# Two loads moved to the queue of ScalarE and a stored Gram block laid out by head, in a kernel of linear attention, soft experts and a feed-forward network

## The chip, the cores and the metric

The kernel runs on one core of one Trainium2 chip. The metric is the time of one launch in device microseconds (us); smaller is better. Three runs of the kernel before took 604.23, 604.43 and 599.4 us (median 604.23). A further execution was recorded by the hardware profiler: 600.38 us, with a span of 598.7 us between its first and last instruction. All rows shown before the result are of that execution.

The engines are TensorE (PE, with its weight loads as PEld), VectorE (DVE), ScalarE (ACT), GpSimd (POOL) and SyncE (SP). SP does no arithmetic here: before the change it issues all DMAs.

## The reference, cut to what matters

Three parts follow one another: a delta-rule attention (4 batches, 8 heads, 768 tokens, head size 48), a soft mixture of experts (8 experts with 4 slots each) and a feed-forward network on 3072 rows.

```python
def _attn_ref(q, k, v, beta):
    k_n = k / (np.linalg.norm(k, axis=-1, keepdims=True) + 1e-06)
    state = np.zeros((B, H, D, D))
    for t in range(S):
        kt, vt, bt = k_n[:, :, t], v[:, :, t], beta[:, :, t, None]
        y[:, :, t] = np.einsum('bhd,bhde->bhe', q[:, :, t], state)
        v_old = np.einsum('bhde,bhd->bhe', state, kt)
        state = state + bt[..., None] * np.einsum('bhd,bhe->bhde', kt, vt - v_old)

def _moe_ref(x, phi, w1, w2):          # x: 3072 x 384
    logits = x @ phi
    d = softmax(logits, axis=0)         # over the tokens
    slot_input = (d.T @ x).reshape(8, 4, 384)
    slot_out[e] = np.maximum(slot_input[e] @ w1[e], 0) @ w2[e]
    return softmax(logits, axis=1) @ slot_out

def _moe2_ref(x, w_in, w_out):
    h = x @ w_in
    return np.maximum(0.01 * h, h) @ w_out
```

## The kernel before, in words

The 768 tokens are cut into 24 chunks of 32, the steps `s` of the loop. All 32 (batch, head) pairs are worked on at once, half of the heads in each of two halves `A`. Inside a chunk the recurrence is a triangular system; its inverse is needed per pair and per chunk. Four chunks make a group `g`.

**Ahead of the recurrence.** `gram(s)` multiplies a chunk's keys with its keys and queries on PE (L189). ACT copies the key part out of PSUM into `gcs` (L196), a tile of one group that lies in the shared buffer `arena`; DVE masks the other part into `mm` (L205). Once the four Gram blocks of a group are there, `solve(g)` transposes the stored copy on DVE so that each pair lies on a partition (L229), eliminates column by column (some 120 short DVE operations, L269, L283 and L287 most of them), transposes back (L290) and stores the inverse as two fp16 parts `tc` (L294 on ACT, L295 on DVE). In the trace these tiles appear as `arena`. Grams run eight chunks ahead of the recurrence; the last is issued in step 15.

**One step of the recurrence.** `ks(A)` on PE (L377) applies the state to the keys, `z_of` splits the result into three fp16 parts (L391 and L392 on ACT, L393 on DVE), `u_mm` multiplies by the inverse `tmb` (L399) and ACT rounds to `u` (L404, then L407 after a correction on PE, L406; from step 17 on DVE L409 does the second part), `s_mm` adds to the state (L420, copied to `st` by ACT, L423), `mu_mm` makes the output `y` (L430), and ACT and DVE store it as `xg` (L736, L737). The next step's `ks(0)` needs `st` of half 0. Beside that, POOL scales the values (`vs`, L327) and splits keys (L337), ACT prepares the keys (L333, L336), and the soft mixture works on groups of finished rows (`soft`, L450 to L503).

**Loads of one step.** All go through SP's queue in the order that the scheduler gives it: the pair of loads `kqb` (keys and queries in block form, 192 KB each, L351), `kv` (keys and values four steps ahead, 384 KB, L304), four copies `tmb` of the inverse (L355), four copies `khb` of the split keys (L344), two `arena` loads and one `kqr` load for the Gram block of ten steps ahead (L172, L178). `kqb`, `tmb` and `khb` have two halves, used by even and odd steps. `load_kv(s + 4, ...)` is held until the last matmul of `u` of half 0. In the later steps weights of the stages behind (768 KB each, L519, L557) are issued on the same queue, each when a slot comes free.

Every DMA takes the next of eight semaphores, whichever queue it is on, and before it is issued it waits until the DMA eight places earlier in the program has landed. An engine works its queue strictly in order, so what stands behind a waiting DMA waits too.

**What sets the order.** A scheduler orders the instructions of each engine from their dependences and a cost estimate; `behind(...)`, `tc.issue_after(...)` and `pri(...)` narrow its choice. Dividing a tile differently or moving a load thus also shifts other instructions.

Of the kernel before, what the change touches and what calls it, by code (L numbers as in the profile page):

```python
# [8 lines left out]
F32 = mybir.dt.float32  # L9
# [3 lines left out]
AF = mybir.ActivationFunctionType  # L13
# [4 lines left out]
NST = 24  # L18
# [29 lines left out]
def fused_kernel(ctx: ExitStack, tc: tile.TileContext, kq, kv, bu, phi, w1, w2, wi, wo, out):  # L48
    nc = tc.nc
    ve, sc, gp, pe, sy = nc.vector, nc.scalar, nc.gpsimd, nc.tensor, nc.sync  # L50
# [15 lines left out]
    kqb = [free_a.tile(KQT, F32, name=f"kqb{i}") for i in range(2)]  # L66
# [29 lines left out]
    def place(kb, shape, dt):  # L96
        n = 1
        for x in shape[1:]:
            n *= x
        n = n // (1 if dt == F32 else 2)  # L100
        v = arena[0:shape[0], 256 * kb:256 * kb + n]
        v = v if dt == F32 else v.bitcast(dt)
        if len(shape) == 2:
            return v
        d = "abcdef"[:len(shape) - 1]
        return v.rearrange(f"p ({' '.join(d)}) -> p {' '.join(d)}", **dict(zip(d, shape[1:])))
# [3 lines left out]
    AT = {"gc": 32, "gu": 44, "R": 48, "tmp": 52}  # L110
# [41 lines left out]
    def behind(*keys):  # L152
        st = ExitStack()
        for k in keys:
            if k in end:
                st.enter_context(tc.issue_after(end[k]))
        return st

    kqc, gcs, mms, tcs, nns, kvs, vns = {}, {}, {}, {}, {}, {}, {}
# [22 lines left out]
    def gram(s, later=None):  # L182
        k = s % 2
        c, kb = kqc[s // 2]
        gp_, tg = ((ps_g, "gm"), (ps_x, "xp"), (ps_y, "y"), (ps_m, "m"))[s % 4 if s < GALT else 0]
        gm = gp_.tile([128, 8, 64], F32, tag=tg, name="gm")
        for h in range(8):
            for bp in range(2):
                end["gm"] = pe.matmul(gm[64 * bp:64 * bp + 64, h, :], kb[:, k, bp, :, h], c[:, k, bp, :, :, h],  # L189
                                      start=(h == 0), stop=True, skip_group_check=True).ins  # L190
            if h % 4 == 3:
                yield
        if s % 4 == 0:
            gcs[s // 4] = place(AT["gc"], [128, 4, 8, 32], F32)
        with behind("nu") if s > 3 else nullcontext():
            gc_ = sc.activation(gcs[s // 4][:, s % 4], gm[:, :, 0:32], AF.Copy).ins  # L196
        if s < 4:
            end["gc"] = gc_
        m = p_mm.tile([128, 2, 32, 4], F32, tag="mm", name="mm")
        mms[s] = m  # L200
        mv = m.rearrange("p a i h -> p a h i")
        gv = gm[:, :, 32:64].rearrange("p (a h) i -> p a h i", a=2)

        def mask():
            ve.tensor_tensor(mv, gv, causal.unsqueeze(1).unsqueeze(1).to_broadcast([128, 2, 4, 32]), MULT)  # L205

        if later is None:
            mask()
        else:
            later.append(mask)  # L210
        yield
# [13 lines left out]
    def solve(g):  # L225
        gc = gcs.pop(g)
        tcg = p_late.tile([128, 4, 4, 2, 32, 4], F16, tag=f"tc{g % 2}", name="tc", bufs=1)
        gu = place(AT["gu"], [128, 32, 32], F32)
        ve.transpose(out=gu, in_=gc.rearrange("p s h i -> p i (s h)"))  # L229
        yield  # L230
        nu, ru, br, er, t0 = [p_gs.tile([128, 32], F32, tag=n, name=n) for n in ("nu", "ru", "br", "er", "t0")]
        nn = p_gs.tile([128, 4, 8], F32, tag="nn", name="nn")
        R = place(AT["R"], [128, 32, 32], F32)
        dg = diag(gu)

        end["t0"] = ve.tensor_scalar(t0, dg, 2.0 ** -63, None, MAX).ins
        sc.activation(nu, t0, AF.Ln)
        end["nu"] = sc.activation(nu, nu, AF.Exp, scale=0.5).ins

        ve.tensor_scalar(er, nu, 2e-6, 1e-12, MULT, ADD)  # L240
        ve.tensor_tensor(er, er, dg, ADD)
        ve.reciprocal(er, er)
        ve.scalar_tensor_tensor(br, er, -1.0, beta[:, g, :], MULT, MULT)
        ve.tensor_scalar(diag(R), br, 64.0, None, MULT)
        nns[g], tcs[g] = nn, tcg
        yield
        for m in (16, 8, 4, 2, 1):
            q = below(AT["gu"], m)
            rows = br.rearrange("p (b x) -> p b x", x=2 * m)[:, :, m:2 * m].unsqueeze(3).to_broadcast([128, 16 // m, m, m])
            ve.tensor_tensor(q, q, rows, MULT)  # L250
            if m > 4:
                yield
        yield
        for m in (16, 8, 4, 2, 1):
            cols = diag(R).rearrange("p (b x) -> p b x", x=2 * m)[:, :, 0:m].unsqueeze(2).to_broadcast([128, 16 // m, m, m])
            ve.tensor_tensor(below(AT["R"], m), below(AT["gu"], m), cols, MULT)
            if m > 4:
                yield

        ve.reciprocal(ru, nu)  # L260
        ve.tensor_tensor(ru, ru, dg, MULT)
        ve.tensor_tensor(nu, nu, ru, ADD)
        ve.tensor_scalar(t0, nu, -32.0, -64e-6, MULT, ADD)
        ve.transpose(out=nn.rearrange("p s h -> p (s h)"), in_=t0)
        yield
        tmp = place(AT["tmp"], [128, 1024], F32)

        def row(i, j):
            ve.scalar_tensor_tensor(R[:, i, 0:j], R[:, j, 0:j], gu[:, i, j:j + 1], R[:, i, 0:j], MULT, ADD)  # L269

        for j in range(1, 31):
            n, w = 30 - j, j
            if w <= COLS:
                for k in reversed(range(w)):
                    ve.scalar_tensor_tensor(R[:, j + 1:, k], gu[:, j + 1:, j], R[:, j, k:k + 1], R[:, j + 1:, k], MULT, ADD)
                yield
            elif n < ROWS:
                for i in range(j + 1, 32):
                    row(i, j)
                yield  # L280
            else:
                tv = tmp[:, 512 * (j % 2):512 * (j % 2) + n * w].rearrange("p (i k) -> p i k", i=n)
                ve.tensor_tensor(tv, gu[:, j + 2:, j:j + 1].to_broadcast([128, n, w]),  # L283
                                 R[:, j:j + 1, 0:w].to_broadcast([128, n, w]), MULT)
                row(j + 1, j)
                yield
                ve.tensor_tensor(R[:, j + 2:, 0:w], R[:, j + 2:, 0:w], tv, ADD)  # L287
                yield
        tt = place(AT["tmp"], [128, 8, 32, 4], F32)
        ve.transpose(out=tt.rearrange("p s i h -> p i s h"), in_=R)  # L290
        tt = tt.rearrange("p (s a) i h -> p s (a i h)", a=2)
        th, tl = [tcg[:, :, i].rearrange("p s a i h -> p s (a i h)") for i in range(2)]
        for k in (slice(0, 1), slice(1, 4)):
            sc.activation(th[:, k], tt[:, k], AF.Copy, scale=2.0 ** -11)  # L294
            solved[g] = ve.scalar_tensor_tensor(tl[:, k], th[:, k], -2048.0, tt[:, k], MULT, ADD).ins  # L295
        yield

    solved = {}

    def load_kv(s, ins=None):  # L300
        p, k = divmod(s, 2)
        if k == 0:
            kvs[p] = p_late.tile([128, 2, 2, 384], F32, tag=f"kv{p % 2}", name="kv", bufs=1)
        d = sy.dma_start(kvs[p][:, k], kv[p, :, k])  # L304
        if ins is not None:
            hold(d, ins)
        return d
# [32 lines left out]
    def step_kdma(s):  # L340
        khc = khs.pop(s)
        for b in range(4):
            q, o = slice(32 * b, 32 * b + 32), 48 * (b % 2)
            last_dma[0] = sy.dma_start(khb[q, s % 2, :, :, b // 2, o:o + 48, :].rearrange("p l a d h -> p (l a) (d h)"), khc[q]).ins  # L344

    def step_dma(s):
        g, k = divmod(s, 4)
        if s:
            for sl in range(2):
                q, i = slice(48 * sl, 48 * sl + 48), slice(32 * sl, 32 * sl + 32)  # L350
                sy.dma_start(kqb[s % 2][q, :, :, i].rearrange("p b x i h -> p (b x) (i h)"),  # L351
                             kq[s // 2, q, s % 2].rearrange("p (c y) -> p c y", c=4))
        for b in range(4):
            q = slice(32 * b, 32 * b + 32)
            sd = sy.dma_start(tmb[s % 2][q, :, :, q, :].rearrange("p l a i h -> p (l a) (i h)"), tcs[g][q, k].rearrange("p l a i h -> p (l a) (i h)"))  # L355
        last_dma[0] = sd.ins
# [9 lines left out]
    last_u = {}  # L366
# [286 lines left out]
    for s in range(NST):  # L653
        y = ps_y.tile([128, 8, 48], F32, tag="y", name="y")
# [3 lines left out]
        def ks(A):  # L658
            if s:
                ks_mm(s, A)  # L660
            z[A] = z_of(s, A) if s else first_z[A]
# [11 lines left out]
                drain(gram(s + GA))  # L673
        with behind("gm", "k"):
            ks(1)
        if s in (3, 7, 11, 15):
            bs.add(solve(s // 4 + 2))
        if s + 1 < NST:
# [22 lines left out]
        with behind("y"):  # L701
# [14 lines left out]
            if s < NST - 1:  # L716
                with pri("st"):
                    s_mm(s, 1, u[1])
        if s + 4 < NST:
            load_kv(s + 4, last_u[0].ins)  # L720
        if s + 1 < NST - 1:
            with pri("dma"):
                step_kdma(s + 1)
# [315 lines left out]
```

## Time and profile before

| | |
|---|---|
| three runs | 599.4, 604.23, 604.43 us |
| profiled execution | 600.38 us, span 598.7 us |
| PE busy over the span | 512.1 us (86%) |
| DVE, ACT, POOL busy | 380.2 us (64%), 297.8 us (50%), 205.4 us (34%) |
| prologue (grams 0 to 7, first solve) | 0 to 58 us |
| 24 attention steps | 58 to 312 us |
| expert weights | 312 to 376 us, DMA 94% busy at 383 GB/s |
| feed-forward network | 376 to 599 us, PE busy 215.6 of 223 us |
| issue to landing, `kqb` / `kv` / `tmb` / `khb` | 5.3 / 4.4 / 3.2 / 3.7 us in the median |

The 24 steps start (store of the previous output on ACT) between 9 and 14 us apart. A step has a chain through all engines, `ks`, `z`, `u`, `st`, and on PE the work that fills the chain's gaps. The chain of waits names for each moment what the end waited for; a busy engine that is not on it costs nothing.

### The profile page before, as it was taken

How to read it: one execution, taken by the hardware profiler on the slowest of the kernel's cores; microseconds unless marked ns; L12 is line 12 of the kernel's file. 1: busy time of each engine (PE TensorE's matmuls, PEld its weight loads, DVE VectorE, ACT ScalarE, POOL GpSimd, SP SyncE). 2: the span in 40 equal slices, each digit the busy share in tenths (PEclk: the TensorE clock that was granted, in tenths of full speed). 3: DMA queues.
4: the chain of work that ended last, by engine and by line, in shares of the span. 5: the costliest groups of instructions: out<-in, count | busy, mean ns of one | idle time of the engine just before them, and what ended most of it. 6: DMA issues, size and time to landing. Idle time of an engine off the chain costs nothing.

```text
span 598.7 us, 20034 instructions
## 1 busy us (share of the span) xinstructions
PE 512.1 (86%) x8368; PEld 376.8 (63%) x8368; DVE 380.2 (64%) x1044; ACT 297.8 (50%) x702; POOL 205.4 (34%) x217
## 2 busy tenths in 40 slices
PE   7705988989999999877666848899999999999996
PEld 5604987988888988776662313565555555555553
DVE  3899988999988989896547560787333333233331
ACT  1312556546655666554433620566655555565552
POOL 9503311321331331521101000355645455555542
PEclk9865988998999999898875959999999999999999
DMA  9964785675787656769899998110101010010101
GB/s 236 251 144 96 158 170 129 168 187 126 184 171 157 158 127 172 168 184 277 181 384 416 412 415 331 54 54 1 53 2 54 0 54 1 2 53 1 54 0 54
DMA packets 71194, 87.37 MB, mean 146 GB/s; under 512 B 42944, under 2 KB 59584, under 8 KB 71104
## 3 DMA queue, kind: packets, MB, share of 16 engines
q1 hardware_dynamic: 71104, 86.09, 51.0%
q8 instruction: 66, 1.08, 0.8%
q14 instruction: 24, 0.20, 0.1%
HBM read 70.53 MB, written 4.72 MB: 126 GB/s over the span
## 4 chain that ended last, share of the span: by engine, by line
PE 64%; DVE 16%; DMA 10%; ACT 4%; issue 3%; SPq 2%; POOL 0%; DVEq 0%; ACTq 0%
PE ops L936 31%; PE gm L189 6%; PE sps L420 5%; DMA arena<-in_w_dram 4%; PE hps L980 3%; DMA we<-in_w_dram 3%; PE ksu L377 2%; PE ksu L369 2%; PE y L430 2%; DVE arena L269 2%; PE ksu L399 2%; DVE arena L283 2%; DVE arena L287 2%; DVE arena L229 2%; PE y L385 1%
## 5 line engine op out<-in xcount | busy, mean ns | idle before, releaser
L992 POOL TENSOR_TENSOR gl<-gf,gh 128x512 f16<-128x512 f32 x96 | 111.9, 1180 | 154.6 <-ACT gh L991 86.4
L936 PE MATMUL ops<-late,gh 128*128 128x384 f16 x768 | 143.6, 326 | 0.1
L986 DVE SCALAR_TENSOR_TENSOR gf<-hps,hs 128x512 f32<-128x512 f32 x96 | 62.6, 686 | 109.8 <-ACT hs L985 109.3
L936 PEld LDWEIGHTS <-gh 128*128 128x128 f16 x768 | 74.8, 98 | 54.8 <-ACT gh L991 1.4
L936 PE MATMUL ops<-late,gl 128*128 128x384 f16 x384 | 81.2, 326 | 0.0
L985 ACT ACTIVATE hs<-hps 128x512 f32<-128x512 f32 x96 | 52.6, 593 | 51.7 <-PE hps L980 51.7
L991 ACT ACTIVATE gh<-gf 128x512 f16<-128x512 f32 x96 | 60.4, 629 | 28.9 <-DVE gf L986 23.9
L327 POOL TENSOR_TENSOR vs<-kv,nn 128x384 f32<-128x384 f32 x24 | 20.7, 861 | 132.4 <-DMA kv<-in_kv_dram 68.3
L420 PE MATMUL sps<-u,khb 128*128 128x48 f16 x1104 | 55.0, 196 | 8.4 <-ACT u L404 4.2
L189 PE MATMUL gm<-kqr,arena 128*64 128x64 f32 x640 | 45.8, 310 | 18.3 <-DVE mm L205 18.3
L420 PEld LDWEIGHTS <-khb 128*128 128x128 f16 x1104 | 51.3, 117 | 13.6 <-issue 12.0
L189 PEld LDWEIGHTS gm<-kqr,arena 128*64 128x64 f32 x640 | 42.2, 221 | 20.9 <-DVE mm L205 18.6
L283 DVE TENSOR_TENSOR arena<-arena 128x81 f32<-128x81 f32 (+12 forms) x150 | 54.5, 363 | 0.1
L936 PEld LDWEIGHTS <-gl 128*128 128x128 f16 x384 | 37.6, 98 | 25.0
L269 DVE SCALAR_TENSOR_TENSOR arena<-arena 128x28 f32<-128x28 f32 (+27 forms) x186 | 51.7, 288 | 0.3
L287 DVE TENSOR_TENSOR arena<-arena 128x81 f32<-128x81 f32 (+12 forms) x150 | 51.5, 343 | 0.0
L430 PE MATMUL y<-u,tmb 128*128 128x48 f16 x576 | 35.8, 197 | 6.6 <-issue 6.5
L404 ACT ACTIVATE u<-ksu 128x192 f16<-128x192 f32 x48 | 15.7, 330 | 41.1 <-PE ksu L399 40.3
L399 PE MATMUL ksu<-z,tmb 128*128 128x48 f16 x576 | 27.4, 193 | 9.1 <-DVE z L393 5.3
L385 PE MATMUL y<-st,kqb 128*32 128x48 f32 x1472 | 29.7, 228 | 6.2 <-issue 5.1
L423 ACT ACTIVATE st<-sps 128x384 f32<-128x384 f32 x46 | 22.4, 492 | 24.9 <-PE sps L420 24.6
L377 PE MATMUL ksu<-st,kqb 128*32 128x48 f32 x1472 | 32.7, 232 | 1.4 <-issue 1.1
(163 smaller groups left out, 862.2 us busy)
## 6 DMA issues: line engine op xcount, KB each, us to landing
we<-in_w_dram SPq DMA_DIRECT2D x22, 768.0 KB, 13.4
kv<-in_kv_dram SPq DMA_DIRECT2D x24, 384.0 KB, 4.4
kqb<-in_kq_dram SPq DMA_DIRECT2D x46, 192.0 KB, 5.3
kqr<-in_kq_dram SPq DMA_DIRECT2D x20, 384.0 KB, 5.7
arena<-in_w_dram SPq DMA_DIRECT2D x10, 768.0 KB, 11.6
tmb<-tc SPq DMA_DIRECT2D x96, 64.0 KB, 3.2
arena<-in_wi_dram SPq DMA_DIRECT2D x8, 768.0 KB, 7.5
raw<-in_wo_dram SPq DMA_DIRECT2D x8, 768.0 KB, 15.1
```

The costliest lines, as they stand in the source:

```text
L189: end["gm"] = pe.matmul(gm[64 * bp:64 * bp + 64, h, :], kb[:, k, bp, :, h], c[:, k, bp, :, :, h], start=(h == 0), stop=True, skip_group_ch ...
L269: ve.scalar_tensor_tensor(R[:, i, 0:j], R[:, j, 0:j], gu[:, i, j:j + 1], R[:, i, 0:j], MULT, ADD)
L283: ve.tensor_tensor(tv, gu[:, j + 2:, j:j + 1].to_broadcast([128, n, w]), R[:, j:j + 1, 0:w].to_broadcast([128, n, w]), MULT)
L287: ve.tensor_tensor(R[:, j + 2:, 0:w], R[:, j + 2:, 0:w], tv, ADD)
L377: end["ks"] = pe.matmul(ksu[A][32 * b:32 * b + 32, 48 * hh:48 * hh + 48], kb[:, bp, 0, r, 4 * A + hh], st[:, bp, hh, :], start=False, stop ...
L420: last_s[0] = pe.matmul(sps[A][:, bp, hh, :], kb[:, a, A, bp, :, hh], u[:, b, hh, :], start=False, stop=(s == NST - 2 and i == 2), skip_gr ...
L430: end["mu"] = pe.matmul(y[:, 4 * A + hh, :], mv[:, a, A, :, hh], u[:, b, hh, :], start=(s == 0 and A == 0 and hh == 0 and i == 0), stop=(i ...
L936: pe.matmul(ops[t], g[:, 128 * t:128 * t + 128], w, start=(ft == 0 and i == 0), stop=(ft == 15 and i == 2))
L985: sc.activation(hs, hps, AF.Copy, scale=2.0 ** -12)
L986: gf_ins = ve.scalar_tensor_tensor(gf, hps, 0.01 * 2.0 ** -12, hs, MULT, MAX).ins
L991: sc.activation(gh, gf, AF.Copy)
L992: gp.tensor_tensor(gl, gf, gh, SUB)
```

## The change

Two edits. First, the stored copy `gcs` has the order [step, row, head] instead of [step, head, row]: ACT writes its 256 values per partition with a stride of 8 values (32 bytes) where it wrote them one after the other, and the transposition L229 reads runs of 8 neighbouring values where it read single values 32 values (128 bytes) apart.

Second, the `kqb` pair of the next step and the `kv` load of four steps ahead are issued by ACT, in program order right behind `z` of half 1, and `kv` is no longer held on the matmuls of `u`. Their sizes are the same.

```diff
-            gcs[s // 4] = place(AT["gc"], [128, 4, 8, 32], F32)
+            gcs[s // 4] = place(AT["gc"], [128, 4, 32, 8], F32)
-            gc_ = sc.activation(gcs[s // 4][:, s % 4], gm[:, :, 0:32], AF.Copy).ins
+            gc_ = sc.activation(gcs[s // 4][:, s % 4].rearrange("p i h -> p h i"), gm[:, :, 0:32], AF.Copy).ins
-        ve.transpose(out=gu, in_=gc.rearrange("p s h i -> p i (s h)"))
+        ve.transpose(out=gu, in_=gc.rearrange("p s i h -> p i s h"))
-    def load_kv(s, ins=None):
+    def load_kv(s, ins=None, eng=sy):
-        d = sy.dma_start(kvs[p][:, k], kv[p, :, k])
+        d = eng.dma_start(kvs[p][:, k], kv[p, :, k])
+    def step_kq(s):
+        for sl in range(2):
+            q, i = slice(48 * sl, 48 * sl + 48), slice(32 * sl, 32 * sl + 32)
+            sc.dma_start(kqb[s % 2][q, :, :, i].rearrange("p b x i h -> p (b x) (i h)"),
+                         kq[s // 2, q, s % 2].rearrange("p (c y) -> p c y", c=4))
     def step_dma(s):
-        if s:
-            for sl in range(2):
-                q, i = slice(48 * sl, 48 * sl + 48), slice(32 * sl, 32 * sl + 32)
-                sy.dma_start(kqb[s % 2][q, :, :, i].rearrange("p b x i h -> p (b x) (i h)"),
-                             kq[s // 2, q, s % 2].rearrange("p (c y) -> p c y", c=4))
         with behind("gm", "k"):
             ks(1)
+        with behind("z"):
+            if s + 1 < NST:
+                step_kq(s + 1)
+            if s + 4 < NST:
+                load_kv(s + 4, eng=sc)
-        if s + 4 < NST:
-            load_kv(s + 4, last_u[0].ins)
```

What the edits make of the order is seen in the built programs. On ACT, in a step with a Gram block (step 10), from the Gram copy to the state copies, before:

```order
L196 ACTIVATE arena<-gm 128x256
L336 ACTIVATE khc<-kv 128x384
L391 ACTIVATE z<-ksu_158 128x192
L392 ACTIVATE z<-ksu_158 128x192
L404 ACTIVATE u<-ksu_157 128x192
L404 ACTIVATE u<-ksu_158 128x192
L407 ACTIVATE u<-ksu_157 128x192
L407 ACTIVATE u<-ksu_158 128x192
```

and now (the lines below the first edits are numbered one higher):

```order
L196 ACTIVATE arena<-gm 128x8x32
L336 ACTIVATE khc<-kv 128x384
L392 ACTIVATE z<-ksu_158 128x192
L393 ACTIVATE z<-ksu_158 128x192
L349 DMA kqb_72<-in_kq_dram 48x4x256 x2
L304 DMA kv<-in_kv_dram 128x768
L405 ACTIVATE u<-ksu_157 128x192
L405 ACTIVATE u<-ksu_158 128x192
L408 ACTIVATE u<-ksu_157 128x192
L408 ACTIVATE u<-ksu_158 128x192
```

Three DMA issues stand between `z` of half 1 and the first `u`; the rest of the order is the same. On SP, the loads of about one step (10 to 11), before:

```order
L304 DMA kv<-in_kv_dram 128x768
L351 DMA kqb_71<-in_kq_dram 48x4x256 x2
L344 DMA khb<-khc 32x4x192
L172 DMA arena<-in_kq_dram 48x2x256 x2
L355 DMA tmb_73<-tc 32x8x128 x4
L344 DMA khb<-khc 32x4x192 x3
L351 DMA kqb_72<-in_kq_dram 48x4x256 x2
L304 DMA kv<-in_kv_dram 128x768
```

and now:

```order
L178 DMA kqr<-in_kq_dram 96x1024
L344 DMA khb<-khc 32x4x192
L172 DMA arena<-in_kq_dram 48x2x256 x2
L356 DMA tmb_73<-tc 32x8x128 x4
L344 DMA khb<-khc 32x4x192 x3
```

The `kqb` and `kv` loads are gone from between the copies; the order of what stays is nearly the same, and SP issues 66 loads fewer over the kernel. On ACT in step 17, from the first `z` to the first `u`, before:

```order
L391 ACTIVATE z<-ksu_157 128x192
L392 ACTIVATE z<-ksu_157 128x192
L320 ACTIVATE tc<-mm 128x256
L333 ACTIVATE kv<-kv 128x384
L499 ACTIVATE ce<-ce 128x128
L336 ACTIVATE khc<-kv 128x384
L391 ACTIVATE z<-ksu_158 128x192
L392 ACTIVATE z<-ksu_158 128x192
L404 ACTIVATE u<-ksu_157 128x192
```

and now:

```order
L500 ACTIVATE ce<-ce 128x128
L392 ACTIVATE z<-ksu_157 128x192
L393 ACTIVATE z<-ksu_157 128x192
L320 ACTIVATE tc<-mm 128x256
L333 ACTIVATE kv<-kv 128x384
L336 ACTIVATE khc<-kv 128x384
L392 ACTIVATE z<-ksu_158 128x192
L393 ACTIVATE z<-ksu_158 128x192
L349 DMA kqb_71<-in_kq_dram 48x4x256 x2
L304 DMA kv<-in_kv_dram 128x768
L405 ACTIVATE u<-ksu_157 128x192
```

The exponential `ce` of the soft mixture, which waits for a POOL operation queued behind `vs`, now stands ahead of both `z`. Elsewhere the operations of the solves on DVE stand somewhat earlier: about 40 in the first step of a group where about 34 stood.

## Rows read from the trace of the kernel before

**Rows 1.** Windows by stage: window, length, busy (count) per engine, clock, DMA share, GB/s.
```profile
58.00:237.00 179.00, 165.89 (x4570) 153.53 (x4569) 161.13 (x561) 104.58 (x303) 47.32 (x61) 0.96 0.69 159
237.00:312.00 75.00, 57.21 (x1743) 52.76 (x1742) 51.71 (x135) 35.03 (x103) 16.50 (x27) 0.89 0.84 233
```

**Rows 2.** Chain of waits, first and last Gram copy and transposition: start, us, what.
```profile
17.15 0.39 ACT arena L196
...
17.57 1.98 DVE arena L229
...
220.05 0.40 ACT arena L196
...
220.98 2.02 DVE arena L229
```

**Rows 3.** Groups by line: line, engine, operation, shapes, count | busy us, mean ns | idle before.
```profile
L229 DVE STREAM_TRANSPOSE arena<-arena 128x1024 f32<-128x1024 f32 x6 | 12.1, 2022 | 1.3 <-ACT arena L196 1.3
L290 DVE STREAM_TRANSPOSE arena<-arena 128x1024 f32<-128x1024 f32 x6 | 7.5, 1245 | 0.2
L196 ACT ACTIVATE arena<-gm 128x256 f32<-128x256 f32 x24 | 9.2, 384 | 33.0 <-PE gm L189 32.9
L985 ACT ACTIVATE hs<-hps 128x512 f32<-128x512 f32 x96 | 52.6, 593 | 51.7 <-PE hps L980 51.7
L819 ACT ACTIVATE cT<-tp 128x512 f16<-128x512 f16 x6 | 8.0, 1330 | 9.2 <-PE tp L817 9.2
L205 DVE TENSOR_TENSOR mm<-gm,causal 128x256 f32<-128x256 f32 x24 | 16.2, 697 | 13.7 <-ACT arena L196 13.5
L393 DVE SCALAR_TENSOR_TENSOR z<-ksu,z 128x192 f16<-128x192 f32 x48 | 16.5, 346 | 3.6 <-ACT z L392 3.5
```

**Rows 4.** Timeline of ACT, steps 9, 12, 17 and 21: start, us, operation, [idle before].
```profile
155.26 0.31 ACT L499 ACTIVATE ce<-ce 128x128 f32<-128x128 f32 x1 [2.15 <-POOL ce L498]
...
189.50 0.33 ACT L392 ACTIVATE z<-ksu 128x192 f16<-128x192 f32 x1
190.78 0.33 ACT L404 ACTIVATE u<-ksu 128x192 f16<-128x192 f32 x1 [0.95 <-PE ksu L399]
191.83 0.33 ACT L404 ACTIVATE u<-ksu 128x192 f16<-128x192 f32 x1 [0.72 <-PE ksu L399]
...
241.67 0.31 ACT L499 ACTIVATE ce<-ce 128x128 f32<-128x128 f32 x1 [2.65 <-POOL ce L498]
...
284.56 0.33 ACT L404 ACTIVATE u<-ksu 128x192 f16<-128x192 f32 x1 [3.01 <-PE ksu L399]
```

**Rows 5.** Timeline of POOL, step 17.
```profile
240.45 0.83 POOL L327 TENSOR_TENSOR vs<-kv,nn 128x384 f32<-128x384 f32 x1 [9.05 <-DMA kv<-in_kv_dram]
```

**Rows 6.** Timeline of PE, start of step 13.
```profile
195.68 0.72 PE L377 MATMUL ksu<-st,kqb 128*32 128x48 f32 x32
```

**Rows 7.** DMA issues of one line each: min/median/max ns on the queue.
```profile
L351 SPq DMA_DIRECT2D kqb<-in_kq_dram x46: 311/442/2219, 28.2 to 292.6; - x46
DMA to landing us min/median/max: 2.8/5.3/9.6
...
L304 SPq DMA_DIRECT2D kv<-in_kv_dram x24: 328/388/652, 8.8 to 260.8; - x24
...
L344 SPq DMA_DIRECT2D khb<-khc x92: 585/599/1804, 32.5 to 291.1; - x92
```

**Rows 8.** Chain of waits, 120 to 160: pieces on SP's queue.
```profile
124.20 0.36 SPq L304
...
126.37 0.43 SPq L351
...
148.88 2.22 SPq L351
```

**Rows 9.** Timeline of SP's queue: start, us, line, loads.
```profile
182.00 0.91 SPq L351 DMA_DIRECT2D kqb<-in_kq_dram  x2
...
284.91 2.56 SPq L355 DMA_DIRECT2D tmb<-tc  x4
...
293.17 5.55 SPq L355 DMA_DIRECT2D tmb<-tc  x4
```

## The prediction

> **What bounds the kernel now.** I read the windows by stage first. From 58 to 237 us, where steps carry Gram blocks and solves, PE is busy 165.9 of 179 us and DVE 161.1; from 237 to 312 both fall to some 57 and 52 of 75 us while the DMA engines rise to a share of 0.84 [rows 1]. So the early steps are bound by work on PE and DVE in turn, the late ones by transfers, and the change touches both. Behind 312 us it touches nothing; what the attention ends earlier or later, the end does too, since the last weights wait for its buffers. I count one for one.
>
> Then the chain of waits, which says where a shorter operation pays. It is made of PE's matmuls for the most part, but it passes through the Gram copy on ACT and the transposition on DVE again and again, from the first (17.15 and 17.57 us) to the last (220.05 and 220.98) [rows 2]. Third the groups by line, for prices [rows 3], and last the timelines around the places that the change moves [rows 4 to 9].
>
> **Part 1, the transposition.** L229 takes 2022 ns; L290, the same operation on as many values, read in order and written in runs of four, takes 1245 ns [rows 3]. The new L229 reads runs of eight and writes in order. Ends: no gain, if a run of eight costs like single values, and 0.78 us. I take 0.78, since L290 is the nearest row. Of the six, five are pieces of the chain, from 17.57 to 220.98 us [rows 2]; the sixth lies beside PE work: 5 x 0.78 = **-3.9 us**; bounds 0 and 6 x 0.78 = -4.7.
>
> **Part 2, the Gram copy.** It writes 256 values with a stride of 32 bytes, and no such ACT row exists. Contiguous it takes 384 ns [rows 3]. One end is +0. For the other, L819 writes 512 values at a stride of 8 bytes in 1330 ns where L985 writes 512 in order in 593: (1330 - 593)/512 = 1.44 ns a value, so 256 x 1.44 = +0.37 us. Between them stands DVE's mask L205, written at a stride of 16 bytes: 697 ns for 256 values, where L393 takes 346 for 192, so at most 346 x 256/192 = 461; at least +0.24. I take +0.28. The chain holds this copy 8 times of 24, the first at 17.15, the last at 220.05 us [rows 2]: 8 x 0.28 = **+2.2 us**; bounds 0 and, at every step, 24 x 0.37 = +8.9.
>
> The nearest strided rows thus make it an addition that eats over half of part 1. The Trainium skill, "SBUF — State Buffer", section "Specifications (TRN2)", speaks the same way against this edit: lines of 16 bytes want two hits each for full speed, and every crossing pays. By that, a 32-byte stride has one hit a line and should be no cheaper than L819's 8-byte stride with two; the sum would be 8 x 0.09 = 0.7 us higher.
>
> **Part 3, three issues on ACT ahead of `u`.** On SP one `kqb` issue takes 442 ns in the median and one `kv` 388 [rows 7]: 2 x 0.44 + 0.39 = 1.27 us. In the step shown `z` of half 1 ends at 189.83 and the first `u` starts at 190.78, after an idle 0.95 us; the second starts at 191.83 after another 0.72 [rows 4]. PE's next matmuls start behind the second, so ACT has 0.95 + 0.72 = 1.67 us for free. 1.27 fits: **0**. The cover goes once the issues take over 1.67 us: a `kqb` issue has taken 2.2 us, and SP's own `khb` issues of 0.6 us stand beside them [rows 7]. This is rival B.
>
> **Part 4, `kqb` closer to its use.** Before, the pair for the step whose `ks` starts at 195.68 [rows 6] was issued at 182.00 [rows 9], 13.7 us ahead. Now the second of the pair is issued at 189.83 + 0.44 = 190.27 and has 195.68 - 190.27 = 5.4 us to land; landing took 2.8/5.3/9.6 us [rows 7]. That is a tie: nearly half of the loads come late, those by a few tenths mostly. With 0.25 us for every second one that is 0.12 us for each of 16 Gram steps: **+2.0 us**; bounds 0 and, were half of the loads late by 1 us, 16 x 0.5 = +8.
>
> **Part 5, `kv` earlier.** POOL's `vs` waits for `kv`, and ACT's `ce` for the POOL operation behind `vs`: at 240.45 `vs` had waited 9.05 us [rows 5], and `ce` held ACT for 2.65 us, ahead of `z` of half 1; at 155.26 for 2.15 [rows 4]. `kv` now starts some 4 us earlier in the step. Where `ce` no longer waits, 2.15 + 2.65 = 4.8 us of ACT come free, of which the chain gets what its other waits leave: I take **-3.0 us** (0.8 and 2.2). What is late next there is `z` on DVE. Bounds 0 and -4.8. In the new order `ce` of step 17 stands ahead of both `z`; should `kv` still be late it holds both, which is why the bound is not passed.
>
> **Part 6, SP's queue.** The chain passes through it at 124 to 128 us, where `khb` stands behind a `kv` issue of 0.36 us and two `kqb` issues of 0.43 each, and at 148.88, a `kqb` issue of 2.22 [rows 8]. Those are removed from it. The latter stands in the same wait as the `ce` at 155.26 and is counted there. **-1.3 us** (0.36 + 2 x 0.43 and the gaps between); bounds 0 and -4.3, with the issues at 148 (0.38 + 0.44 + 2.22) on top. In other steps SP's queue is ahead of its users, and the relief is worth nothing.
>
> **Part 7, late steps.** Each DMA waits for the one eight places back. In steps 20 to 22 the places eight back of ACT's `kqb` pair are `khb` and `tmb` copies that SP issues behind 768 KB weights, and `u` now stands behind them. In step 21, `tmb` for the next step was issued from 284.91 on [rows 9] and lands about 3.2 us after issue; the second of the four, at 285.55, at 288.7. `u` went at 284.56 [rows 4]: 4.1 us later, half of it hidden by the wait for weights that ends step 21 anyway: +2. In step 22 `tmb` was issued at 293.17, taking 5.55 us for four [rows 9]; PE waited there until 299.03 already, so `u`, `st` behind it and the copies add about +1.5. Step 20: `khb` landings, +1. Sum **+4.5 us**; bounds 0 (SP's queue moves ahead as well) and +8.
>
> Other edits of the order: DVE's solve work stands earlier, beside the same PE work; what hides it is the Gram block. If that cover were gone, six operations of 0.3 us more ahead of `z` cost 1.8 us in a step, in the two first steps of a group; I take 0.
>
> **Sum.** -3.9 + 2.2 + 0 + 2.0 - 3.0 - 1.3 + 4.5 = +0.5. Against the profiled execution, 600.38 + 0.5 = 600.9, so **601 us**. That execution lies 3.9 us under the median of the three runs (604.23) and 1 us over the lowest; I state the time on its level.
>
> **Rival A, faster: SP's queue was the limiter.** If ACT's issues stay inside their cover and the late waits have landed by then, part 7 and part 4 are 0, and parts 5 and 6 reach their ends: 600.4 - 3.9 + 2.2 - 4.8 - 4.3 = **590 us** (589.6). For it: the chain goes through SP's queue in two of its long holds [rows 8]. Against: it does so in few of the 24 steps. The skill weighs in against it: "DMA: Bandwidth & Descriptors", section "Issuing engines are not separate DMA queues", says that loads begun on several engines share the same 16 engines and that only issue time is saved. By that no landing gets shorter and this rival keeps only the issue times, 0.36 to 2.22 us apiece, of part 6; the late stage at a DMA share of 0.84 [rows 1] agrees that the transfers are the scarce thing there.
>
> **Rival B, slower: ACT is held in order by its issues.** An issue on ACT may take as long again as the `khb` issue beside it: 1.27 + 3 x 0.6 = 3.1 us, 1.4 over the free 1.67, and `u`, `st` and the next `ks` are late by that. It decides from 1.67 us on between `z` and `u`. In half of 16 Gram steps that is 8 x 1.4 = 11 us: 601 + 11 = **612 us**. For it: issues of `kqb` range from 311 to 2219 ns [rows 7], and SP keeps all its copies to issue. Against: three issues of median length fit.
>
> **Rival C, the moves do nothing.** The loads were hidden before and stay hidden; only parts 1 and 2 remain: 600.4 - 3.9 + 2.2 = **599 us**, inside the forecast's 1%.
>
> **How the numbers follow.** Chances: forecast 0.32, A 0.28, B 0.29, C 0.11. About 1% (6 us) is what a measurement of this kernel tells from no change. Faster by over 1%: A and some of the forecast's and C's lower ends, 0.32. Slower by over 1%: B and the forecast's upper end (part 4 at +8, part 7 at +8), 0.30. Within: 0.38. The range takes in A and B with what lies just around them: 589 to 614 us. The likeliest case alone, with the bounds of parts 4 and 7, spans 595 to 610.
>
> **What would show it.** Part 1: L229 at about 1245 ns instead of 2022. Part 2: L196 between 384 and 750 ns. Part 3: the idle time of ACT before the first `u` smaller by the issues, the second `u` as long after `z` as before; for B, PE waiting on `u` at its state matmuls. Part 4: `ks` of half 0 or its weight loads waiting for `kqb`. Part 5: POOL's wait for `kv` down from the 9.05 us, and no 2 us waits at `ce`. Part 7: ACT's queue standing at the `kqb` issue in steps 20 to 22, with `u` behind it. The prediction is wrong if the issues on ACT take over 1.67 us in most steps, or if the solve's new places on DVE set the step.

## The result: slower by 0.9%, where 601 us and "no change" stood likeliest

The changed kernel took 607.15 us in the median of 20 runs, the kernel before 602.59 in 20 runs; the ratio is 1.0091 (above 1 is slower), 95% interval [1.0067, 1.0115], some 5.5 us. Every ratio here is the recorded one, of fast runs alone, and differs by up to 0.4% from the quotient of the medians of all runs (here 1.0076, 4.6 us). The time is inside the predicted range, but a slowdown clear of the noise was measured where "no change" stood likeliest. The execution that the profiler recorded took 602.18 us (span 600.5), the lowest of the 20, so its rows show less of the loss than the runs do. Where it matters I compare rows of several kernels, not this one pair alone; each kernel has one profiled execution.

The two prices of the layout came out as taken. Groups by line of the profile after (the same columns as in [rows 3]; line numbers are up to four higher):

```profile
L229 DVE STREAM_TRANSPOSE arena<-arena 128x1024 f32<-128x1024 f32 x6 | 7.4, 1232 | 1.3 <-ACT arena L196 1.3
L196 ACT ACTIVATE arena<-gm 128x256 f32<-128x256 f32 x24 | 15.6, 649 | 32.8 <-PE gm L189 32.8
```

The transposition fell from 2022 to 1232 ns, the copy rose from 384 to 649 ns (+0.265, where +0.28 was taken). The issues on ScalarE, min/median/max in ns on the queue, and their landing:

```profile
L349 ACTq DMA_DIRECT2D kqb<-in_kq_dram x46: 317/344/1932, 32.1 to 299.0; - x46
...
DMA to landing us min/median/max: 2.9/4.1/7.3
```

An issue costs 0.34 us in the median, less than on SP, and the pair lands in 4.1 us instead of 5.3 [rows 7]; `kv` lands in 5.9 us instead of 4.4.

The stages, columns as in [rows 1], cut where ScalarE stores the outputs of steps 0, 16, 20 and 23 (L736, now L740). So the three rows are steps 1 to 16 (Gram blocks and most of the solves), 17 to 20, and 21 to 23. Before:

```profile
58.57:236.48 177.91, 164.80 (x4544) 152.53 (x4544) 160.04 (x555) 103.53 (x301) 47.32 (x61) 0.97 0.69 158
236.48:277.80 41.32, 33.29 (x1024) 30.76 (x1024) 35.32 (x98) 22.78 (x67) 13.23 (x17) 0.93 0.80 205
277.80:312.00 34.20, 24.44 (x731) 22.42 (x729) 16.91 (x38) 12.74 (x40) 3.27 (x10) 0.85 0.90 268
```

and after:

```profile
57.25:237.51 180.26, 164.04 (x4543) 152.00 (x4543) 157.31 (x555) 106.27 (x302) 48.70 (x61) 0.96 0.68 158
237.51:282.27 44.76, 35.27 (x1024) 32.59 (x1023) 34.25 (x98) 22.84 (x67) 14.27 (x17) 0.84 0.72 187
282.27:316.33 34.06, 24.21 (x739) 22.53 (x738) 18.38 (x39) 13.55 (x41) 2.92 (x10) 0.88 0.86 290
```

In this pair, steps 1 to 16 take 2.3 us longer and steps 17 to 20 take 3.4; steps 21 to 23 take as long as before. In steps 17 to 20 PE is also busy for longer with as many matmuls: 35.27 us at a mean granted clock of 0.84 (full speed is 1), where it was 33.29 at 0.93. Over all 23 steps that is 1.0 us (223.5 against 222.5); the rest of the 5.7 us that they take longer is idle time. Of the 4.3 us by which the last step ends later (the first starts 1.3 earlier), this execution gets 2.5 back behind it.

What changed most is who waits for whom on TensorE. Waits of PE from 58 to 312 us (waiting line <- what it waited for: us in total, times, longest), first before:

```profile
PE y L430 <- issue: 6.5, 3, 4.3
PE ksu L399 <- DVE z L393: 5.3, 9, 1.8
PE y L385 <- issue: 5.1, 5, 1.7
PE ksu L399 <- DMA tmb<-tc: 2.3, 1, 2.3
PE sps L420 <- ACT u L404: 2.2, 2, 2.0
PE sps L420 <- ACT u L407: 1.7, 5, 0.4
```

and after:

```profile
PE ksu L400 <- DVE z L394: 13.7, 20, 2.2
PE sps L421 <- ACT u L405: 3.7, 6, 1.4
PE y L386 <- DVE xg L741: 3.3, 3, 2.8
PE sps L421 <- ACT u L408: 3.0, 11, 0.7
PE lp L450 <- DVE acc L492: 2.8, 1, 2.8
...
PE ksu L378 <- DMA kqb<-in_kq_dram: 0.7, 1, 0.7
```

The inverse's matmuls wait for VectorE's part of `z` 8.4 us more; the state matmuls wait for ScalarE's `u` 2.8 us more (3.7 + 3.0 against 2.2 + 1.7); the close landing of `kqb` cost 0.7 us once. VectorE has become what is late most often. But other waits went: those that end with nothing that the profile shows (`issue`), 14 us before, are nearly gone. The waits of this view add up to 29.1 us before and 32.4 after, 3.3 us more, so the 8.4 us are not by themselves the loss.

One such wait is step 3 (VectorE's timeline, then TensorE's; start, us, operation, [idle before]):

```profile
85.14 1.25 DVE L290 STREAM_TRANSPOSE arena<-arena 128x1024 f32<-128x1024 f32 x1
86.31 1.20 DVE L229 STREAM_TRANSPOSE arena<-arena 128x1024 f32<-128x1024 f32 x1
87.44 0.32 DVE L394 SCALAR_TENSOR_TENSOR z<-ksu,z 128x192 f16<-128x192 f32 x1
```

```profile
87.81 0.56 PE L400 MATMUL ksu<-z,tmb 128*128 128x48 f16 x12 [2.23 <-DVE z L394]
```

Before, the same two transpositions stood behind `z` of half 1 in this step (`z` at 87.08, L290 at 89.12). Now the solve runs some operations earlier, both stand ahead of `z`, and PE waits 2.23 us.

The late steps have two more places. In step 20 ScalarE stands at the `kqb` issue, as part 7 said (ScalarE, then TensorE):

```profile
275.52 0.32 ACT L393 ACTIVATE z<-ksu 128x192 f16<-128x192 f32 x1
277.51 1.06 ACTq L349 DMA_DIRECT2D kqb<-in_kq_dram  x2
278.67 0.55 ACT L405 ACTIVATE u<-ksu 128x192 f16<-128x192 f32 x2 [2.83 <-DMA khb<-khc]
```

```profile
279.05 0.35 PE L421 MATMUL sps<-u,khb 128*128 128x48 f16 x4 [1.42 <-ACT u L405]
```

`z` was done at 275.84, the issue waited until 277.51 (for a `khb` landing, by the profile), `u` stood behind it, and PE idled 1.42 us. In steps 21 to 23 something else stands first: a weight conversion (L527) is ahead of both `z`, and in step 21 also the soft mixture's `ce` (ScalarE, step 21):

```profile
282.27 0.50 ACT L740 ACTIVATE xg<-y 128x384 f16<-128x384 f32 x1
...
286.26 0.84 ACT L527 ACTIVATE arena<-arena 128x768 f16<-128x768 f32 x1 [2.38 <-DVE arena L514]
287.47 0.31 ACT L500 ACTIVATE ce<-ce 128x128 f32<-128x128 f32 x1 [0.36 <-POOL ce L499]
287.69 0.31 ACT L392 ACTIVATE z<-ksu 128x192 f16<-128x192 f32 x1
```

From the store of the output to the end of the first `z` it takes 5.95 us here (288.22 - 282.27); in step 21 before, without such an operation ahead, 2.6 (277.80 to 280.38). No DMA issue is in it. All the same these three steps together took no longer than before in this pair (34.06 against 34.20 us).

### The profile page after: what moved, and what is told of

It reads as the page before. It is cut to its first block, busy times and chain, and to the rows that moved or that the text cites. A ratio compares the mean times of both kernels' runs of the same rounds, so it can differ in the third digit from the quotient of the medians.

```text
span 600.5 us, 19990 instructions
## 1 busy us (share of the span) xinstructions
PE 513.6 (86%) x8368; PEld 378.1 (63%) x8368; DVE 375.2 (62%) x1044; ACT 302.3 (50%) x702; POOL 207.7 (35%) x217
## 4 chain that ended last, share of the span: by engine, by line
PE 55%; DVE 24%; DMA 11%; ACT 4%; issue 3%; SPq 1%; ACTq 0%; DVEq 0%
PE ops L940 31%; DMA arena<-in_w_dram 5%; DVE arena L283 4%; DVE arena L287 4%; PE gm L189 4%; DVE arena L269 4%; PE sps L421 4%; PE hps L984 3%; DMA arena<-in_wi_dram 3%; DMA we<-in_w_dram 3%; PE y L431 2%; PE ksu L370 2%; PE hn L842 1%; PE ksu L378 1%; PE gpsum L927 1%
## 5 line engine op out<-in xcount | busy, mean ns | idle before, releaser
L327 POOL TENSOR_TENSOR vs<-kv,nn 128x384 f32<-128x384 f32 x24 | 21.9, 911 | 112.4 <-PE ksu L370 63.4
L269 DVE SCALAR_TENSOR_TENSOR arena<-arena 128x28 f32<-128x28 f32 (+27 forms) x186 | 49.9, 278 | 0.4
L400 PE MATMUL ksu<-z,tmb 128*128 128x48 f16 x576 | 27.4, 194 | 13.8 <-DVE z L394 13.7
L400 PEld LDWEIGHTS <-tmb 128*128 128x128 f16 x576 | 24.9, 118 | 16.9 <-issue 15.5
```

What stands on the lines that cost most here:

```text
L400: last_u[A] = pe.matmul(ksu[A][:, 256 + 48 * hh:304 + 48 * hh], tmb[s % 2][:, a, A, :, hh], z[:, b, 48 * hh:48 * hh + 48], start=False, st ...
```

## The experiments

Theory 1: moving the loads makes the scheduler give other engines a new order (solves packed earlier on VectorE, so that more of their operations fall into one step; later operations ahead of `z` on ScalarE), and that order costs the time. Theory 2: the three issues, or the waits in front of them, hold ScalarE ahead of `u`. Theory 3: the slower Gram copy costs it. Diffs are cut to what matters. All ratios are against runs of the kernel before on the same chip.

### e1: the layout alone

The three lines of the diff that concern `gcs`, nothing else.

> The layout edit alone, all loads on SP's queue as before; the order of every engine stays that of the kernel before. Theory 1 (the move of the loads makes the scheduler pack the solves on VectorE, and z waits for them) and theory 2 (ACT is held by the issues ahead of u): 1 to 4 us faster than before, ratio 0.993 to 0.998, with L229 near 1232 ns and the Gram copy near 650 ns. Theory 3 (the slower Gram copy is what costs): slower, ratio 1.003 to 1.010.

Measured: 599.33 against 600.11 us, ratio 1.0012 [0.9978, 1.0047]. Neither a gain nor a loss that can be told. Theory 3 falls as the cause of 0.9%; the gain of 0.3% that parts 1 and 2 left is not seen either.

### e2: the move of the loads alone

The diff without the three `gcs` lines.

> The move of the loads alone, the Gram block stored as before; every engine's order is that of the changed kernel. Theories 1 and 2: slower than before by 6 to 9 us, ratio 1.010 to 1.015, more than the changed kernel's 1.009. Theory 3: within 0.3% of before.

Measured: 607.18 us, ratio 1.0154 [1.0109, 1.0199]. The move alone loses. With the layout on top it is 1.0091, so on the new order the layout seems to help (the two intervals overlap at their ends only); on the old one it does not (e1).

### e3: the new places, on SP's queue

```diff
-            sc.dma_start(kqb[s % 2][q, :, :, i].rearrange("p b x i h -> p (b x) (i h)"),
+            sy.dma_start(kqb[s % 2][q, :, :, i].rearrange("p b x i h -> p (b x) (i h)"),
-                load_kv(s + 4, eng=sc)
+                load_kv(s + 4)
```

> The changed kernel with both loads at their new place in the program, but issued by SP; VectorE's order is again that of the kernel before up to step 20. Theory 1 and theory 2 both: the loss goes, ratio 0.993 to 0.999. If the loss lies in the loads' new place in the step (kqb too close to its use, kv no longer held), whichever queue issues them: ratio near 1.009 as the changed kernel's.

Measured: 597.23 us, ratio 0.9983 [0.9953, 1.0013]. The places in the program cost nothing; it takes ScalarE's queue, by its order or by its issues, to lose. Theories 1 and 2 remain.

### e4 and e8: only `kv` on ScalarE, with and without the layout

`step_kq` is taken out and the `kqb` pair is back in `step_dma` on SP; `load_kv(s + 4, eng=sc)` stays behind `z`.

> Layout edit, and only the kv load issued by ACT behind z; the kqb pair stays on SP. VectorE's order is that of the kernel before. Theory 1: no loss, ratio 0.992 to 0.999. Theory 2: one of three issues stands ahead of u, so a third of its loss remains, ratio about 1.000 to 1.004.

> Only the kv load moved to ACT, Gram block stored as before. If kv alone is the gain of e4 (0.9945) and the layout gives nothing (e1: 1.001): 0.993 to 0.997. If the layout gives its 0.6% as it did between e2 and the changed kernel: 0.999 to 1.003.

Measured: e4 596.50 us, ratio 0.9945 [0.9903, 0.9987]; e8 594.13 us, ratio 0.9902 [0.9864, 0.9939], the fastest kernel of this study, faster than the kernel before and the changed one. One issue ahead of `u` costs nothing that can be told, and moving `kv` is worth 0.6 to 1.0%. What went are GpSimd's waits for `kv`. Waits ahead of `vs` (L327) in e8, in all, against 68.3 us in 10 waits for `kv` before:

```profile
  PE ksu L372: 85.0, 14
...
  DMA kv<-in_kv_dram: 3.8, 1
```

With `vs` in time, ScalarE hardly waits at `ce` for the POOL operation behind it; its waits there, before and in e8:

```profile
  POOL ce L498: 5.1, 3
```

```profile
  POOL ce L501: 0.4, 1
```

Step 17 in e8 and, in [rows 5], before:

```profile
230.86 0.83 POOL L327 TENSOR_TENSOR vs<-kv,nn 128x384 f32<-128x384 f32 x1 [5.48 <-PE ksu L372]
```

`vs` now waits until TensorE has released its buffer, not for its data. Between the output stores of steps 0 and 16 lie 171.9 us in e8 (58.46 to 230.40) and 177.9 before (58.57 to 236.48). That the 1% comes of these waits is argued, not shown. Nor is `kv`'s new place alone known to give it: e3 has `kv` there on SP's queue, and its 0.9983 is no gain that can be told. So taking `kv` off SP's queue may be part of it.

### e5: only the `kqb` pair on ScalarE

```diff
-            if s + 4 < NST:
-                load_kv(s + 4, eng=sc)
...
+        if s + 4 < NST:
+            load_kv(s + 4, last_u[0].ins)
```

> Layout edit and only the kqb pair issued by ACT behind z; kv stays on SP, held on u as before. VectorE's order is near that of the kernel before (28 to 33 solve operations in a step, as there). Theory 1 (packed solves on VectorE): no loss, ratio 0.996 to 1.002. Theory 2 (ACT held ahead of u): two of three issues and all late waits remain, ratio 1.004 to 1.009.

Measured: 598.67 against 600.43 us, ratio 0.9975 [0.9944, 1.0007]. Two of the three issues and every late wait of the pair stand ahead of `u` here, and in all nothing is lost. VectorE's order is nearly that of before. This speaks against theory 2 as the main cause. It doesn't make the pair free: PE waits 3.8 us for late `kqb` landings here, all in the late steps, which it never did before.

### e6: the packed order without any issue on ScalarE

e3, with `z` and the output store on VectorE held behind a number of solve operations that is read off the changed kernel's order:

```diff
+    def mark(f):
+        while len(ops) < AHEAD[len(at_mark)] and bs.q:
+            bs.run(1)
+        k = min(AHEAD[len(at_mark)], len(ops))
+        at_mark.append(k)
+        with tc.issue_after(ops[k - 1]):
+            return f().ins
-        end["zd"] = ve.scalar_tensor_tensor(z[:, 1], zp, 2.0 ** -6, z[:, 0], MULT, SUB).ins
+        end["zd"] = mark(lambda: ve.scalar_tensor_tensor(z[:, 1], zp, 2.0 ** -6, z[:, 0], MULT, SUB))
```

> All loads on SP as in e3, but VectorE's z and output operations are held behind as many solve operations as in the changed kernel (33 to 35, then 43 and 40 in two steps, then 20). Theory 1: the loss comes back without any issue on ACT, ratio 1.004 to 1.015. Theory 2: as e3, ratio 0.995 to 1.002. Orders of TensorE and ScalarE also follow, so a loss here shows the packing, not every detail of it.

Measured: 611.03 us, ratio 1.0168 [1.0125, 1.0211], a little above what was expected. Busy time from 58 to 237 us, columns as in [rows 1]:

```profile
58.00:237.00 179.00, 157.85 (x4266) 144.65 (x4265) 146.96 (x510) 100.66 (x283) 45.96 (x58) 0.95 0.66 149
```

PE does 157.85 us of work in a stretch in which it did 165.89 before. So a held order can cost more than the whole loss without any issue on ScalarE. It isn't a copy of the changed kernel: TensorE's order became its own, and PE's waits in this stretch are more for ScalarE's `u` (6.1 + 2.5 us) than for VectorE's `z` (7.0). So neither the size nor the share of `z` carries over.

### e7: the issues on ScalarE, the solves unpacked

The changed kernel, where each solve operation is issued behind the `z` or store that it followed before (as far as that one is written ahead of it in the program):

```diff
+            k = sum(1 for x in SOLVE_AT if x <= self.n)
+            self.n += 1
+            k = min(k, len(self.marks))
...
+            with self.tc.issue_after(self.marks[k - 1]):
+                return f(*a, **kw)
```

> The changed kernel, all three issues on ACT, but each solve operation on VectorE may not stand ahead of the z or output operation that it followed in the kernel before; TensorE's order stays near the changed kernel's. Theory 1: half the loss or more goes, ratio 0.997 to 1.004 against 1.009. Theory 2: the loss stays, 1.007 to 1.012.

Measured: 605.22 against 600.43 us, ratio 1.0045 [1.0010, 1.0081]. By the ratios about half of the loss goes, but the interval touches the changed kernel's, and the quotient of the medians is 1.0080. PE's waits for VectorE's `z`, 58 to 237 us, changed kernel and e7:

```profile
PE ksu L400 <- DVE z L394: 8.1, 14, 2.2
```

```profile
PE ksu L425 <- DVE z L418: 4.5, 12, 1.6
```

They fall from 8.1 to 4.5 us (2.1 before). Yet steps 1 to 16 of this profiled execution are no shorter (181.2 us against 180.3), and from 58 to 312 us PE waits 7.5 us for `kqb` landings, where it waited 0.7 in the changed kernel. The restriction doesn't restore the old order: two steps still have 42 and 44 solve operations.

### e9: conversions behind `z` in the late steps

```diff
-                with pri("wi"), tc.issue_after(solved[NG - 1]):
+                with pri("wi"), tc.issue_after(solved[NG - 1]), behind("z"):
```

> The changed kernel with one restriction: the weight conversions of the late steps may not be issued before z of half 1 of their step; on ScalarE they then stand behind z instead of ahead of it in steps 21 to 23, the rest of the order is nearly the changed kernel's. If the loss comes from what the new order puts ahead of z (theory 1, widened to ScalarE's late steps): 2 to 5 us less than the changed kernel, ratio 1.001 to 1.006. If it is the issues and waits ahead of u (theory 2): no change, 1.008 to 1.012.

Measured: 604.91 against 601.01 us, ratio 1.0058 [1.0039, 1.0076]. By the ratios, one restriction on the conversions takes a third of the loss (1.0091 - 1.0058 = 0.33%, some 2 us) with all three issues where they were. The intervals overlap, so it is a sign and no proof; in the profiled execution steps 21 to 23 take 32.7 us instead of 34.1.

### e10: three issues of `kv`, the `kqb` pair on SP

```diff
+            for j, lo, hi in ((0, 0, 384), (1, 0, 192), (1, 192, 384)):
+                d = eng.dma_start(kvs[p][:, k, j, lo:hi], kv[p, :, k, j, lo:hi])
```

> e8 with the kv load cut into three issues on ScalarE of the same bytes in all; the kqb pair stays on SP, so none of its waits or landings is touched, and the Gram block is stored as before. The scheduler then packs the solves as in the changed kernel. If it is the third issue and the order that it brings (theories 1 and 2 in the Gram steps): the gain of e8 (0.990) goes, ratio 0.997 to 1.012. If the loss lay in the kqb pair's landing or its waits in the late steps: 0.988 to 0.995.

Measured: 606.63 us, ratio 1.0093 [1.0068, 1.0118]; with one issue for the same bytes (e8) it was 0.9902. No `kqb` is moved here, so the pair's new place cannot be the cause. PE's waits for `z` from 58 to 312 us are near those of the changed kernel, at `u` those of the kernel before (2.0 + 1.9 against 2.2 + 1.7):

```profile
PE ksu L406 <- DVE z L400: 12.2, 14, 1.8
```

It is the cut into three that brings a new order, and with it the loss. But the waits for `z` are only a part of it. Steps 1 to 16, then 17 to 20:

```profile
58.48:234.01 175.53, 162.09 (x4545) 150.69 (x4545) 158.77 (x557) 102.84 (x301) 48.34 (x61) 0.99 0.71 160
234.01:285.37 51.36, 35.67 (x1025) 32.92 (x1025) 35.43 (x101) 22.73 (x67) 13.32 (x17) 0.80 0.72 187
```

Against e8, steps 1 to 16 take 3.6 us more (175.5 against 171.9), about what PE waits more for `z` from 58 to 237 us (8.0 against 4.1). Steps 17 to 20 take 10.7 us more (51.4 against 40.7). There, in step 20, PE stood for 4.03 us in the middle of `ks` for nothing that the profile shows, and for 3.34 us at a `u` of VectorE that stood behind a weight conversion (L517), which had waited 4.65 us for its load. PE, then VectorE:

```profile
275.42 0.31 PE L384 MATMUL ksu<-st,kqb 128*32 128x48 f32 x2 [4.03 <-issue]
```

```profile
283.09 0.56 DVE L517 TENSOR_SCALAR arena<-arena 128x768 uint32<-128x768 uint32 x1 [4.65 <-DMA arena<-in_wi_dram]
283.57 0.35 DVE L416 SCALAR_TENSOR_TENSOR u<-ksu,u 128x192 f16<-128x192 f32 x1
```

Neither has to do with a solve ahead of `z`.

### e11 and e12: the `kqb` pair at other places on ScalarE

e11 loads the pair of two steps ahead behind the store of the output; e12 the pair of the next step behind `z` of half 0. `kv` stays behind `z` of half 1 in both, and the Gram block is stored as before.

```diff
+        if s + 2 < NST:
+            with behind("x"):
+                step_kq(s + 2)          # e11
```

```diff
         with behind("mu", "lp", "x"):
             ks(0)
+        with behind("z"):
+            if s + 1 < NST:
+                step_kq(s + 1)          # e12
```

> All three loads on ScalarE as in the change, Gram block stored as before; kv behind z, but the kqb pair of two steps ahead behind the store of the output, at the end of the step. The order of VectorE and TensorE is near that of the kernel before but for one step with 46 solve operations. Theory 1: 0.988 to 0.997. Theory 2 (any three issues of ScalarE in a step cost, late waits for places eight back too): 1.000 to 1.010.

> All three loads on ScalarE, Gram block stored as before; the kqb pair behind z of half 0, so that only kv stands between z of half 1 and u, and the pair has some 3 us more to land. VectorE's solves are packed as in the changed kernel (33 to 35, then 42 in a step). Theory 1: slower than before, 1.003 to 1.015. Theory 2 or late landings of kqb: most of the loss goes, 0.990 to 1.000.

Measured: e11 597.09 us, ratio 0.9951 [0.9927, 0.9976]; e12 609.96 us, ratio 1.0150 [1.0128, 1.0173]. Both have three issues of ScalarE in a step. With an order near that of before it is faster than before; with the pair moved away from `u` and given more time to land, but with packed solves and an order of its own on TensorE, slower than the changed kernel. What the issues cost by themselves decides neither. In e12 it is not VectorE alone either: from 58 to 237 us PE waits 5.2 us for `z` and 9.5 us for `u`,

```profile
PE sps L421 <- ACT u L408: 7.4, 18, 0.4
...
PE sps L421 <- ACT u L405: 2.1, 5, 0.4
```

and ahead of each of these `u` ScalarE sat idle until TensorE's own matmul (L400 or L407) was done. So in e12 these waits come of TensorE's order.

### e13: both orders undone

e7 and e9 together.

> The restrictions of e7 (solve operations no earlier than in the kernel before) and of e9 (conversions behind z) together; the three issues stay on ScalarE ahead of u. Each took 0.3 to 0.5% off the changed kernel's 1.009. If order alone is the cause they add up: 0.997 to 1.003. If the issues themselves hold ScalarE (theory 2): a floor of 1.004 or more stays.

Measured: 601.38 against 598.97 us, ratio 1.0040 [1.0005, 1.0075]. The two do not add up: the point lies at the floor that was named for theory 2, the interval covers both. So the two restrictions together take some 0.5%; by the two intervals it can be little, or nearly all of the loss. The trace shows where the rest lies (steps 1 to 16, then 17 to 20, and PE's waits for `kqb` over the steps):

```profile
57.99:235.11 177.12, 163.49 (x4543) 151.83 (x4542) 157.94 (x556) 105.80 (x301) 48.39 (x61) 0.97 0.70 161
235.11:279.46 44.35, 36.88 (x1028) 33.78 (x1027) 33.55 (x97) 23.03 (x67) 14.19 (x17) 0.81 0.73 187
```

```profile
PE ksu L402 <- DMA kqb<-in_kq_dram: 5.2, 3, 3.0
```

Steps 1 to 16 are no longer than before (177.1 against 177.9 us). Steps 17 to 20 still are, by 3.0 us, and PE is busy there for 3.6 us more with nearly as many matmuls, at a granted clock of 0.81 where it was 0.93. And PE waits 5.2 us for `kqb`, which it never did before: the late waits that theory 2 names, and not VectorE's order. How the rest divides between the two isn't shown.

## Why the prediction was wrong, step by step

- **The step that failed** is the last line of the parts: "DVE's solve work stands earlier, beside the same PE work; what hides it is the Gram block ... I take 0." The Gram block does not hide it. From 58 to 237 us, where the solves stand, PE's wait for `z` from VectorE went from 2.1 us in 5 waits to 8.1 in 14, and over all steps from 5.3 in 9 to 13.7 in 20. The same step covered ScalarE's order only at one place (`ce` in step 17); the conversions ahead of `z` in steps 21 to 23 stood in the new order too, and I did not price them. That the order, in the main, loses the time, and not the layout or the new places, is supported by e1, e3, e8 against e10, and e11 against e12. How much of the 5.5 us is VectorE's order is not shown: between the profiled executions of e8 and e10 lie 12.9 us, of which steps 1 to 16, where the waits for `z` grew by as much, make 3.6; in e7 fewer such waits made no shorter steps; and in e12 PE waits more for `u`, by TensorE's own order.
- **What no part looked at** is how long TensorE is busy with the same matmuls. Over the 23 steps it was 222.5 us before, 223.5 in the changed kernel, 226.0 in e13 and 226.3 in e7. In steps 17 to 20 the granted clock is lower with it (0.93 before, 0.84, 0.81 and 0.90), but e7 has 35.2 us at 0.90 where the changed kernel has 35.3 at 0.84, so the clock is not all of it. Whether this is a cause of the loss or comes of the new order stays open.
- **Rival B** had the sign and the wrong mechanism: ScalarE held by its issues. They take 0.34 us in the median. PE waits 2.8 us more for `u` in the whole kernel, where 11 was priced; e5 and e11 lose nothing with two or three issues. It is refuted as the main cause, not as a part of the rest of e13.
- **Part 1** was right in its mechanism and size per operation (0.79 us against 0.78), **part 2** too (0.265 against 0.28). Their sum, -1.7 us, was not found by itself: e1 measures +0.1% with an interval of 0.35% to either side.
- By the 16-byte lines of the Trainium skill, "SBUF — State Buffer", section "Specifications (TRN2)", the 32-byte stride should be no cheaper than L819's 8-byte one. Measured: (649 - 384)/256 = 1.04 ns a value against 1.44. The trace doesn't bear that out across these two rows (one writes f32, one f16); its direction, that the stride costs and that runs of eight repair the read, it does.
- **Part 3** held: the issues fit between `z` and `u` in most steps. **Part 4** came out smaller: +2.0 against 0.7 us of waits for `kqb` in `ks`, since the pair lands in 4.1 us. It was partly hidden by the other waits: in e7 and e13, where PE waits less for `z`, it waits 7.5 and 5.2 us for the pair, most of that in the late steps.
- **Part 5** had the right sign: -3.0, bounded at -4.8, where e4 gives 0.55% (3 us) and e8 1.0% (6 us). Its mechanism is seen (the waits of `ce` for GpSimd went from 5.1 to 0.4 us), but not shown to be the whole of the gain. I priced two waits of `ce`, but `vs` waited for `kv` ten times. In the changed kernel much of it is lost again: `vs` waits 25.4 us for `kv`, in 4 waits.
- **Part 6** and rival A: with the pair off SP's queue (e5) the ratio is 0.9975, with all loads on it at the new places (e3) 0.9983. Taking the pair off SP gives nothing that can be told; whether taking `kv` off it is part of e8's gain stays open. The Trainium skill, "DMA: Bandwidth & Descriptors", section "Issuing engines are not separate DMA queues", says that the engines' loads share the same 16 DMA engines. The trace agrees so far: `kqb` lands in 4.1 us from ScalarE, but in 4.4 from SP at the same place in the program (e3), and `kv` lands later than before (5.9 us against 4.4).
- **Part 7** was right in step 20 (1.42 us of PE for the +1 taken) and not seen as such in 21 and 22, where the conversion ahead of `z` comes first and PE waits 0.22 us for `u` at most.

## What to carry to other kernels

Where a scheduler sets the order, an edit is two edits: what it does, and the order that it brings on engines that it does not touch. Price the second from the waits of before: where the rows show someone waiting for an operation already, there is no slack, and what is put ahead of it costs its length. Elsewhere ask how long the slack is (here 9 waits became 20). Then look whether the time of the steps follows: a wait that grows at one place can shrink at another, as it did here. And split a change before keeping or dropping it: here one of three issues gave 0.6 to 1.0%, and the other two, harmless by themselves, took it and as much again.

## What was not expected of the hardware

The shorter landing of `kqb` (46 issues of 192 KB) is not ScalarE's alone. It was 5.3 us before; at its new place it is 4.1 us from ScalarE (issue 344 ns in the median, before 442 on SP), and from SP 4.4 us in e3 (issue 388 ns) and 5.1 in e6, where the order is another:

```profile
kqb<-in_kq_dram SPq DMA_DIRECT2D x46, 192.0 KB, 4.4
```

`kv`, issued by ScalarE right behind that pair, landed later than before (4.4); alone, in e8, it took 4.1 us:

```profile
kv<-in_kv_dram ACTq DMA_DIRECT2D x20, 384.0 KB, 5.9
```

Cutting its 384 KB into three issues on the same queue (e10) left the landing of the two pieces of 96 KB at 3.9 us each in the median, and of the one of 192 KB at 3.4.
